# Making the 8-to-16 doubling's sums by two accumulating transfers, with other vector work between it and the next doubling

## The chip, the cores and the metric

The kernel runs on one core of one Trainium2 chip. A core has five engines that run side by side, each through its own list of instructions in order: TensorE (PE, matrix products), VectorE (DVE, elementwise work), ScalarE (ACT, activations), GpSimd (POOL, elementwise work and the issue of some transfers) and SyncE (SP, which issues most transfers). They wait for each other by semaphores. The metric is the device time of one execution in microseconds. Less is better.

## The reference

Two layers, each a state-space convolution and a gated feed-forward network, act on x of shape 1 x 2048 x 512:

```python
def _A_ref(u, A_re, A_im, B_re, B_im, C_re, C_im, log_dt, Dskip):
    dt = jnp.exp(log_dt)[:, None]
    A, Bc, Cc = A_re + 1j * A_im, B_re + 1j * B_im, C_re + 1j * C_im
    P = jnp.exp((dt * A)[:, :, None] * jnp.arange(L)[None, None, :])      # (512, 128, 2048)
    K = jnp.einsum("dn,dnl,dn->dl", Cc, P, dt * Bc).real                  # convolution kernel
    ...                                          # y = causal convolution of u with K, by FFT
    return y + u * Dskip[None, None, :]

def _B_ref(x, w_gate, w_up, w_down):
    return (_silu(x @ w_gate) * (x @ w_up)) @ w_down

for _ in range(2):
    x = x + _A_ref(_layernorm(x), ...)
    x = x + _B_ref(_layernorm(x), ...)
```

What the change touches is the making of K, the 2048 taps of 512 filters out of 128 complex exponentials each. It is done once and used by both layers.

## The kernel before

**Stages.** The first stage, some 320 us, makes K and its spectra. The rest, which this change does not edit, is eight blocks (two layers of four blocks of 512 rows) of convolution by spectra (`ssm`) and feed-forward network (`ffn`).

**How K is made.** The 512 filters are split into eight chunks of 64. A lag l is written as 32a + b. For one chunk the *large factor* is the power with exponent 32a (tiles `re`, `im` of 65 columns and `mu`), and the *small factor* is the power with exponent b times the coefficient (tile `g`, 128 x 2 x 32 x 64: real and imaginary part, 32 powers, 64 filters). `lags` multiplies the two on PE (lines 509 and 510, 128 small products a chunk into `pk`), ACT copies the result to `ks` (line 515), `spread` lays it out (525, 527, result `kp`), ACT copies that to `kt` (1001), and `spectra` turns it into spectra (`pw`, 546), which ACT (555, tile `s`), POOL (557 and 563) and SP (569) store.

**The parts on the vector engine, chunk by chunk.** Each is a Python generator that gives up control at every `yield`:

- `gen_turns` (365, 368) and `gen_reduce` (`rd`; ACT lines 376 and 382, then DVE lines 385 and 388) form the angles of a chunk and take off whole turns, which leaves a remainder. Line 388 is six instructions, for 16, 8, 4, 2, 1 and 1 powers. This is the "remainder work" and belongs to the chunk two ahead.
- `gen_trig` (ACT lines 395, 396, 397) takes sine and cosine of these remainders in three groups: first `xr`, `xi`, which need 385; then the group of 16 powers, which needs the first 388; then the rest, which needs the other five. `gen_exp` and `gen_mags` (ACT 405 and 441) make the magnitudes.
- `gen_e` (`ge`; 450, 450, 453, 453, 456, 459, 459) builds the large factor of the next chunk.
- `gen_g` (`gg`) builds the small factor of the next chunk by doubling. From power 1 it forms powers 2 to 4 (477 to 481), then from 4 powers 8 and from 8 powers 16 (485 to 489, once for n = 4 and once for n = 8), then from 16 powers 32 (492 to 499). One doubling is a complex product: g times the real part of a step factor, plus the other half of g times its imaginary part (tile `btl`). Up to 16 powers, DVE makes the two sums itself (488, 489). In the last doubling, POOL issues two transfers that add a product tile onto `g` in memory (494 and 499).

**What sets the order.** Between lines 899 and 1100 the instructions of ACT, DVE and PE run in the order in which the Python code issues them. Loop 958 goes over the chunks: iteration i multiplies chunk i on PE, builds `g` and the large factor of chunk i + 1 and the remainders of chunk i + 2 on DVE. The tuple in line 986 says how the generators take turns there. Before the loop, chunk 0 has a tuple of its own (line 929). POOL and SP, and all engines after line 1100, are ordered by a scheduler that works from its own model of times.

Of the kernel before, what the change touches and what calls it, by code (L numbers as in the profile page):

```python
# [16 lines left out]
OP = mybir.AluOpType  # L17
# [64 lines left out]
def kernel(ctx, tc, x, a_re, a_im, b_re, b_im, c_re, c_im, log_dt, d_skip,  # L82
                           w_gate, w_up, w_down, c_ef, c_ei, c_ek, c_am, c_eh, c_eih, out):
    nc = tc.nc
    V, A, G, PE = nc.vector, nc.scalar, nc.gpsimd, nc.tensor
# [9 lines left out]
    def tl(shape, name, tag, dt=F32):  # L95
        return sb.tile(shape, dt, name=name, tag=tag, bufs=BUFS[tag])
# [347 lines left out]
    def gen_e(ts):  # L444


        re, im, mu = ts[:3]
        half = [[t.rearrange("p (g h d) a -> p g h d a", g=4, h=2)[:, :, o] for t in ts[:3]] for o in range(2)]
        for r, m, u in half:
            V.tensor_tensor(m[..., :32], m[..., 64:32:-1], r[..., :32], OP.mult)  # L450
            yield
        for r, m, u in half:
            V.tensor_tensor(r[..., :32], r[..., 64:32:-1], r[..., :32], OP.mult)
            yield
        yield
        V.scalar_tensor_tensor(im[:, :, 33:64], im[:, :, 33:64], -1.0, mu[:, :, 1:], OP.mult, OP.mult)
        yield
        for r, m, u in half:
            V.tensor_tensor(r[..., 33:64], r[..., 33:64], u[..., 1:], OP.mult)
            yield  # L460

    def gen_g(ch, ts, g):

        re, im, mu, xz, mz, t16 = ts
        w_ = w0[:, :, ch * DC:(ch + 1) * DC]
        for t in xz:
            V.tensor_tensor(t, t, mz, OP.mult)
        yield
        tm, th_ = tmp
        V.tensor_tensor(g[:, :, 0], w_, re[:, :, 64].unsqueeze(1).to_broadcast([P, 2, DC]), OP.mult)  # L470
        V.tensor_tensor(tm[:, :, 0], w_[:, ::-1], im[:, :, 64].unsqueeze(1).to_broadcast([P, 2, DC]), OP.mult)
        yield
        V.tensor_tensor(g[:, 0, 0], g[:, 0, 0], tm[:, 0, 0], OP.subtract)
        V.tensor_tensor(g[:, 1, 0], g[:, 1, 0], tm[:, 1, 0], OP.add)
        yield
        zr, zi = (t[:, :3].unsqueeze(1).to_broadcast([P, 2, 3, DC]) for t in xz)
        V.tensor_tensor(g[:, :, 1:4], g[:, :, 0:1].to_broadcast([P, 2, 3, DC]), zr, OP.mult)
        V.tensor_tensor(tm[:, :, :3], g[:, ::-1, 0:1].to_broadcast([P, 2, 3, DC]), zi, OP.mult)
        yield
        V.tensor_tensor(g[:, 0, 1:4], g[:, 0, 1:4], tm[:, 0, :3], OP.subtract)  # L480
        V.tensor_tensor(g[:, 1, 1:4], g[:, 1, 1:4], tm[:, 1, :3], OP.add)
        for n in (4, 8):
            yield
            zr, zi = (t[:, ZP.index(n)].unsqueeze(1).unsqueeze(1).to_broadcast([P, 2, n, DC]) for t in xz)
            V.tensor_tensor(g[:, :, n:2 * n], g[:, :, 0:n], zr, OP.mult)
            V.tensor_tensor(tm[:, :, :n], g[:, ::-1, 0:n], zi, OP.mult)
            yield
            V.tensor_tensor(g[:, 0, n:2 * n], g[:, 0, n:2 * n], tm[:, 0, :n], OP.subtract)
            V.tensor_tensor(g[:, 1, n:2 * n], g[:, 1, n:2 * n], tm[:, 1, :n], OP.add)
        yield  # L490
        zr, zi = (t[:, NZ - 1:].to_broadcast([P, 16, DC]) for t in xz)
        V.tensor_tensor(g[:, 1, 16:], g[:, 1, :16], zr, OP.mult)
        V.tensor_tensor(th_, g[:, 0, :16], zi, OP.mult)
        G.dma_start(g[:, 1, 16:], th_, accum_op=OP.add)
        yield
        tl_ = tm.rearrange("p i s d -> p (i s) d")
        V.tensor_tensor(g[:, 0, 16:], g[:, 0, :16], zr, OP.mult)
        V.scalar_tensor_tensor(tl_, g[:, 1, :16], -1.0, zi, OP.mult, OP.mult)
        G.dma_start(g[:, 0, 16:], tl_, accum_op=OP.add)
        yield  # L500
# [12 lines left out]
    def spread_in(pk):  # L513
        ks = tl([P, 4, 16, 16], "ks", "nn")
        A.activation(ks, pk.rearrange("p d (c a) -> p a c d", a=4), AF.Copy)
        return ks
# [78 lines left out]
    def take(it, n):  # L595
        for _ in range(n):
            next(it, None)
# [301 lines left out]
    with tc.manual_schedule(engines={mybir.EngineType.Activation, mybir.EngineType.DVE, mybir.EngineType.PE}):  # L899
# [19 lines left out]
        gg = gen_g(0, ts[0], gs[0])  # L919
        ge, tn, rd = gen_e(ts[0]), gen_turns(1, ts[1]), gen_reduce(ts[1])  # L920
# [37 lines left out]
        for i in range(NCH - 1):  # L958
            if mags:
                take(mags, 1)  # L960
            pk = lags(ts[i], gs[i])
            more = i + 2 < NCH
            tn = rd = f = iter(())
            if more:
                ts[i + 2] = gen_tiles(i + 2)
                tn = gen_turns(i + 2, ts[i + 2])
            gs[i + 1] = tl([P, 2, 32, DC], "g", ("gb", "ga")[i % 2])
            gg, ge = gen_g(i + 1, ts[i + 1], gs[i + 1]), gen_e(ts[i + 1])
            take(ex, 100)
            if mags:  # L970
                take(mags, 2)
            take(sp, 2)
            norm_units(3, 9)
            norm_units(0, 0)
            ks = spread_in(pk)
            if mags:
                take(mags, 1)
            if i % 2 == 0 and 0 < i < NCH - 2:
                parts(i + 2)
                turned()  # L980
            for g in (gg, tn, gg, tn):
                take(g, 1)
            if more:
                rd = gen_reduce(ts[i + 2])
                next(rd)
            for g in (gg, gg, ge, gg, ge, gg, gg, rd, rd, ge, rd, rd, ge, rd, rd, rd, rd):
                take(g, 1)
            while tops:
                tops.pop(0)()
            take(sp, 1)  # L990
            take(gg, 2)
            kp = spread(i, ks)
            if more:
                f = second(*sec[i])
                next(f)
            take(gg, 2)
            if more:
                tr = gen_trig(ts[i + 2])
                take(tr, 1)
            kt = kt2[:, 0]  # L1000
            A.activation(kt, kp, AF.Copy)
            take(tr, 1)
            take(f, 1)
            take(tr, 1)
            if more:
                sp = spectra(i, kt, 0, NB)
                take(sp, 1)
                ex = gen_exp(i + 2, ts[i + 2])
                take(ex, 100)
                mags = gen_mags(i + 2, ts[i + 2])  # L1010
                take(mags, 2)
                norm_units(3, 9)
                take(sp, 2)
                norm_units(0, 0)
                take(mags, 2)
                take(sp, 2)
                sizes(i, kt, ks)
                take(ge, 4)
                take(gg, 1)
                while tops:  # L1020
                    tops.pop(0)()
                ts[i] = gs[i] = None
            else:
                sizes(i, kt, ks)
                take(ge, 4)
                take(gg, 1)
# [119 lines left out]
```

## Time and profile before

| what | value |
|---|---|
| median of three runs | 1188.11 us (1188.05 to 1190.89) |
| the profiled execution, its own time | 1194.56 us |
| its span in the profile | 1192.8 us |
| busy: PE, DVE, ACT, POOL | 1108.3, 1026.5, 618.0, 185.0 us |
| stage that makes K: chunk 0 alone | about 0 to 57 us |
| loop over the chunks, by the start of `lags` on PE | 58.64, 93.04, 124.39, 155.46, 188.23, 219.15, 250.62 us |

The profile is of one execution. A row of its timeline gives a start, a duration, the engine, the line, the operation, output<-input, and in brackets how long the engine was idle before it and who released it. Durations of one engine overlap a little, because an instruction starts before the one ahead has drained, so the step from one start to the next is what an instruction costs in a row. A row of the waits gives who waited for whom, the total in us, the number of times and the longest one. A row of the transfers gives the number, the size of one and the median time from issue to landing.

### The profile page before, as it was taken

What the parts mean: (1) busy time and instruction counts of PE and PEld (TensorE: products, weight loads), DVE (VectorE), ACT (ScalarE), POOL (GpSimd) and SP (SyncE); (2) the same over time, 40 slices, a digit from 0 to 9 for tenths busy, and PEclk for the clock granted to TensorE, in tenths of its full rate; (3) what the DMA queues carried; (4) which work ended last, traced back from release to release, by engine and by line L of the source; (5) the groups of instructions that cost most, each with busy time, mean ns of one, the idle gap of its engine ahead of it and who ended that gap; (6) DMA issues with size and microseconds to landing.
All of it is one profiled execution on the core that took longest, in us unless ns stands there. A gap on an engine that the chain in (4) does not pass through costs nothing.

```text
span 1192.8 us, 25266 instructions
## 1 busy us (share of the span) xinstructions
PE 1108.3 (93%) x10268; PEld 861.2 (72%) x10268; DVE 1026.5 (86%) x1621; ACT 618.0 (52%) x1166; POOL 185.0 (16%) x238
## 2 busy tenths in 40 slices
PE   2889999889887989999999999999999999999998
PEld 2767776667875767768677787868687686867875
DVE  7989999997879999999999999999992899983211
ACT  6998887862355544537743523655432553224211
POOL 3105454343310011202100000211000010000000
PEclk9989999999989999999999999999999999999999
DMA  6444445577497326432344354324434134312000
GB/s 234 141 107 127 114 119 127 126 181 201 141 297 221 109 89 163 161 111 89 85 152 146 115 165 142 111 81 150 140 123 133 45 115 128 125 46 45 15 23 18
DMA packets 139031, 147.95 MB, mean 124 GB/s; under 512 B 77921, under 2 KB 87137, under 8 KB 138914
## 3 DMA queue, kind: packets, MB, share of 16 engines
q1 hardware_dynamic: 134050, 129.56, 35.8%
q0 software_dynamic: 4864, 16.78, 5.9%
q8 instruction: 80, 1.31, 0.5%
q14 instruction: 37, 0.30, 0.1%
HBM read 99.24 MB, written 28.31 MB: 107 GB/s over the span
## 4 chain that ended last, share of the span: by engine, by line
PE 35%; DVE 26%; issue 5%; ACT 3%; DMA 2%; POOL 2%; SPq 1%; DVEq 0%; ACTq 0%; POOLq 0%
PE pgu L860 6%; PE pgu L861 6%; PE pgu L862 6%; DVE t L736 4%; PE py L874 4%; PE py L875 4%; PE py L876 3%; DVE yk L739 3%; DVE yk L736 3%; PE pi L755 3%; PE pf L270 2%; DVE z L226 2%; DVE sg L866 2%; POOL rs L221 2%; DVE bt L226 1%
## 5 line engine op out<-in xcount | busy, mean ns | idle before, releaser
L860 PE MATMUL pgu<-mix,wsl 128*128 128x256 f16 x1280 | 350.2, 274 | 5.3 <-DVE sg L866 3.6
L862 PE MATMUL pgu<-mix,wsl 128*128 128x256 f16 x1280 | 350.3, 274 | 3.6 <-DVE wsl L632 3.6
L861 PE MATMUL pgu<-mix,wsl 128*128 128x256 f16 x1280 | 350.2, 274 | 0.0
L874 PE MATMUL py<-wsl,hh 128*128 128x512 f16 (+1 forms) x352 | 135.5, 385 | 8.9 <-DVE sgr L836 3.1
L861 PEld LDWEIGHTS <-wsl 128*128 128x128 f16 x1280 | 125.7, 98 | 21.8 <-issue 5.8
L862 PEld LDWEIGHTS <-wsl 128*128 128x128 f16 x1280 | 125.7, 98 | 19.1 <-DVE wsl L632 3.9
L860 PEld LDWEIGHTS <-wsl 128*128 128x128 f16 x1280 | 125.7, 98 | 15.8
L876 PE MATMUL py<-wsl,hl 128*128 128x512 f16 (+1 forms) x352 | 135.2, 384 | 1.3 <-DVE hl L868 1.3
L865 ACT ACTIVATE sg<-pgu,sc 128x512 f32<-128x512 f32 x80 | 54.5, 682 | 135.4 <-PE pgu L862 116.5
L736 DVE TENSOR_TENSOR t<-uu,w 128x1024 f32<-128x1024 f32 x96 | 117.0, 1219 | 8.2 <-DMA uu<-udr 7.9
L875 PE MATMUL py<-wsl,hh 128*128 128x512 f16 x320 | 123.3, 385 | 0.0
L739 DVE TENSOR_TENSOR yk<-yk,t 128x1024 f32<-128x1024 f32 x96 | 116.9, 1218 | 0.2
L866 DVE SCALAR_TENSOR_TENSOR sg<-pgu,sc,sg 128x512 f32<-128x512 f32 x80 | 59.7, 746 | 51.0 <-ACT sg L865 50.8
L546 PE MATMUL pw<-kt,ek 128*128 128x256 f32 (+2 forms) x420 | 98.6, 373 | 0.0
L755 PE MATMUL pi<-yl,mix 128*128 128x256 f16 x672 | 91.4, 273 | 1.7 <-ACT yl L744 1.4
L546 PEld LDWEIGHTS pw<-kt,ek 128*128 128x128 f32 x420 | 78.7, 195 | 9.5
L867 ACT ACTIVATE hh<-sg 128x512 f16<-128x512 f32 x80 | 50.0, 625 | 57.5 <-DVE sg L866 57.4
L221 POOL TENSOR_TENSOR rs<-mv,mhalf 128x2 f32<-128x2 f32 (+1 forms) x21 | 38.3, 1824 | 263.2 <-ACT mv L220 255.8
L270 PE MATMUL pf<-z,eh 128*128 128x256 f16 x576 | 74.6, 273 | 1.4 <-ACT z L260 1.4
L755 PEld LDWEIGHTS <-mix 128*128 128x128 f16 x672 | 65.2, 98 | 13.0 <-issue 2.0
L736 DVE TENSOR_TENSOR yk<-u,w0r 128x1024 f32<-128x1024 f32 x56 | 68.2, 1218 | 0.3 <-ACT u L272 0.3
L875 PEld LDWEIGHTS <-hh 128*128 128x128 f16 (+1 forms) x352 | 34.8, 99 | 46.2 <-issue 11.7
(240 smaller groups left out, 2245.8 us busy)
## 6 DMA issues: line engine op xcount, KB each, us to landing
w<-wdr SPq DMA_DIRECT2D x96, 256.0 KB, 2.7
uu<-udr SPq DMA_DIRECT2D x96, 256.0 KB, 3.0
udr<-u POOLq DMA_DIRECT2D x32, 256.0 KB, 2.9
wdr<-wo SPq DMA_DIRECT2D x96, 64.0 KB, 2.5
udr<-u SPq DMA_DIRECT2D x16, 256.0 KB, 2.2
g<-tmp POOLq DMA_DIRECT2D x8, 512.0 KB, 4.5
g<-btl POOLq DMA_DIRECT2D x8, 512.0 KB, 5.9
n<-ndr SPq DMA_DIRECT2D x16, 256.0 KB, 3.0
```

What stands on the lines that cost most here:

```text
L270: PE.matmul(pf[:, o], lhsT=e, rhs=m, start=k == 0, stop=k == len(terms) - 1)
L546: PE.matmul(pw[:, i], lhsT=e, rhs=kt[:, :, c + 4 * k0:4 * k1:4, :].rearrange("p g k d -> p k g d"), start=c == 0, stop=c == 3)
L736: V.tensor_tensor(t, uu.unsqueeze(1).to_broadcast([P, 2, 2, HD]), w.unsqueeze(2).to_broadcast([P, 2, 2, HD]), OP.mult)
L739: V.tensor_tensor(yk, yk, t, OP.add)
L755: PE.matmul(pi[:, o], lhsT=e, rhs=m, start=k == 0, stop=k == len(terms) - 1)
L860: PE.matmul(o, lhsT=wgu(wi, k, 0)[:, fs], rhs=nh[:, k], start=k == 0, stop=False)
L861: PE.matmul(o, lhsT=wgu(wi, k, 0)[:, fs], rhs=nlo[:, k], start=False, stop=False)
L862: PE.matmul(o, lhsT=wgu(wi, k, 1)[:, fs], rhs=nh[:, k], start=False, stop=k == 3)
L866: V.scalar_tensor_tensor(sg, pgu[:, 1], sc6[:, 4:5], sg, OP.mult, OP.mult)
L874: PE.matmul(py[:, r], lhsT=hh[:n, f, rc], rhs=wd(f, 0)[:n], start=f == 0, stop=False)
L875: PE.matmul(py[:, r], lhsT=hh[:n, f, rc], rhs=wd(f, 1)[:n], start=False, stop=False)
L876: PE.matmul(py[:, r], lhsT=hl[:n, f, rc], rhs=wd(f, 0)[:n], start=False, stop=f == FT - 1)
```

## The change

Only the doubling from 8 to 16 powers and its place change. Where DVE made two products of 128 x 1024 and two sums of 128 x 512, it now makes four products of 128 x 512, and POOL issues two transfers of 256 KB that add the product tile `btl` onto the upper half of `g`, as in the last doubling. In the loop, this doubling moves ahead of the remainder work, and one step each of the large factor's work (the second line 450, the second line 453) moves behind parts of the remainder work. Both steps of the last doubling now stand ahead of `spread`; before, the 8-to-16 doubling stood there. The generator has one step less, so the tuple of chunk 0 (line 929), which is not edited, takes its steps otherwise too. The lines of the new kernel are 486 to 491 for the new doubling and 500 to 507 for the last one, which was 492 to 499.

```diff
         for n in (4, 8):
             yield
             zr, zi = (t[:, ZP.index(n)].unsqueeze(1).unsqueeze(1).to_broadcast([P, 2, n, DC]) for t in xz)
+            if n == 8:
+                V.tensor_tensor(g[:, 1, 8:16], g[:, 1, :8], zr[:, 1], OP.mult)
+                V.tensor_tensor(tm[:, 1], g[:, 0, :8], zi[:, 1], OP.mult)
+                G.dma_start(g[:, 1, 8:16], tm[:, 1], accum_op=OP.add)
+                V.tensor_tensor(g[:, 0, 8:16], g[:, 0, :8], zr[:, 0], OP.mult)
+                V.scalar_tensor_tensor(tm[:, 0], g[:, 1, :8], -1.0, zi[:, 0], OP.mult, OP.mult)
+                G.dma_start(g[:, 0, 8:16], tm[:, 0], accum_op=OP.add)
+                continue
...
-            for g in (gg, gg, ge, gg, ge, gg, gg, rd, rd, ge, rd, rd, ge, rd, rd, rd, rd):
+            for g in (gg, gg, ge, gg, gg, gg, gg, rd, rd, ge, rd, rd, ge, rd, rd, rd, rd, ge):
                 take(g, 1)
...
-            take(gg, 2)
```

Chunk 0, ahead of the loop, on DVE before (`g` is the small factor, `btl` and `tmp` are product tiles, `im` the remainders of chunk 1, `t_171` its angles):

```order
L385 TENSOR_TENSOR xi<-xi,xr 128x384
L485 TENSOR_TENSOR g<-g,xr 128x2x512
L486 TENSOR_TENSOR btl<-g,xi 128x1024
L388 SCALAR_TENSOR_TENSOR im<-t_171,re 128x64x16
L488 TENSOR_TENSOR g<-g,btl 128x512
L489 TENSOR_TENSOR g<-g,btl 128x512
L388 SCALAR_TENSOR_TENSOR im<-t_171,re 128x64x8
L492 TENSOR_TENSOR g<-g,xr 128x1024
L493 TENSOR_TENSOR tmp<-g,xi 128x1024
L388 SCALAR_TENSOR_TENSOR im<-t_171,re 128x64x4
L497 TENSOR_TENSOR g<-g,xr 128x1024
L498 SCALAR_TENSOR_TENSOR btl<-g,xi 128x1024
```

The same place with the change:

```order
L385 TENSOR_TENSOR xi<-xi,xr 128x384
L486 TENSOR_TENSOR g<-g,xr 128x512
L487 TENSOR_TENSOR btl<-g,xi 128x512
L489 TENSOR_TENSOR g<-g,xr 128x512
L490 SCALAR_TENSOR_TENSOR btl<-g,xi 128x512
L388 SCALAR_TENSOR_TENSOR im<-t_171,re 128x64x16
L500 TENSOR_TENSOR g<-g,xr 128x1024
L501 TENSOR_TENSOR tmp<-g,xi 128x1024
L388 SCALAR_TENSOR_TENSOR im<-t_171,re 128x64x8
L505 TENSOR_TENSOR g<-g,xr 128x1024
L506 SCALAR_TENSOR_TENSOR btl<-g,xi 128x1024
L388 SCALAR_TENSOR_TENSOR im<-t_171,re 128x64x4
```

Here only one instruction, the first line 388, stands between the new doubling and the last one. The new L500 waits for the first of the two transfers, L501 for the second.

In the loop, iteration 1 (chunk 2's small factor), on DVE before:

```order
L385 TENSOR_TENSOR xi<-xi,xr 128x384
L388 SCALAR_TENSOR_TENSOR im<-t_972,re 128x64x16
L453 TENSOR_TENSOR re<-re 128x4x8x32
L388 SCALAR_TENSOR_TENSOR im<-t_972,re 128x64x8
L388 SCALAR_TENSOR_TENSOR im<-t_972,re 128x64x4
L453 TENSOR_TENSOR re<-re 128x4x8x32
L388 SCALAR_TENSOR_TENSOR im<-t_972,re 128x64x2
L388 SCALAR_TENSOR_TENSOR im<-t_972,re 128x64 x2
L485 TENSOR_TENSOR g<-g,xr 128x2x512
L486 TENSOR_TENSOR btl<-g,xi 128x1024
L488 TENSOR_TENSOR g<-g,btl 128x512
L489 TENSOR_TENSOR g<-g,btl 128x512
```

The same place with the change:

```order
L489 TENSOR_TENSOR g<-g,xr 128x512
L490 SCALAR_TENSOR_TENSOR btl<-g,xi 128x512
L385 TENSOR_TENSOR xi<-xi,xr 128x384
L388 SCALAR_TENSOR_TENSOR im<-t_976,re 128x64x16
L450 TENSOR_TENSOR im<-im,re 128x4x8x32
L388 SCALAR_TENSOR_TENSOR im<-t_976,re 128x64x8
L388 SCALAR_TENSOR_TENSOR im<-t_976,re 128x64x4
L453 TENSOR_TENSOR re<-re 128x4x8x32
L388 SCALAR_TENSOR_TENSOR im<-t_976,re 128x64x2
L388 SCALAR_TENSOR_TENSOR im<-t_976,re 128x64 x2
L453 TENSOR_TENSOR re<-re 128x4x8x32
L500 TENSOR_TENSOR g<-g,xr 128x1024
```

The new doubling has moved ahead of line 385, and ten instructions stand between it and the last doubling.

On POOL with the change, the same iteration (`s_982` and `s_1059` are the third and the fourth spectrum of the chunk before):

```order
L565 COPY w0r<-s_982 128x2x64
L571 TENSOR_TENSOR wo<-s_982 128x192 x2
L488 DMA g<-btl 128x512
L491 DMA g<-btl 128x512
L407 MEMSET re 128x64
L369 MEMSET im 128x64
L565 COPY w0r<-s_1059 128x2x64
L571 TENSOR_TENSOR wo<-s_1059 128x192 x2
L502 DMA g<-tmp 128x1024
L507 DMA g<-btl 128x1024
```

The two new issues stand behind the third spectrum's work and ahead of the fourth's. ACT and PE keep their order in this whole stage, and SP does but for a few neighbouring transfers. In the later blocks the scheduler, whose model sees other times, has exchanged some neighbouring instructions of all engines but POOL.

## The prediction

> **What bounds the kernel now.** I read the busy time by stage first, since the change lies in the stage that makes K. The row gives window, length, then busy time (and instructions) of PE, weight loads, DVE, ACT, POOL, then the PE clock and the transfers' share. The window is about one turn of the loop, from one start of `lags` to the next.
>
> ```profile
> 92.00:124.00 32.00, 29.00 (x395) 22.11 (x394) 31.07 (x38) 26.89 (x43) 16.96 (x21) 1.00 0.52 125
> ```
>
> DVE is busy 31.07 of 32 us, PE 29.00 and ACT 26.89. From this alone, DVE sets the pace. But a busy engine is not yet one that others wait for. So the second view is who waited for whom: ACT from 51 to 249 us (first four rows), PE from 69 to 249 us (two rows), DVE from 57 to 274 us (last four).
>
> ```profile
> ACT ks L515 <- PE pk L510: 15.4, 5, 3.5
> ACT mu L441 <- PE pm L438: 8.4, 5, 3.0
> ACT re L441 <- PE pm L438: 2.2, 6, 0.4
> ACT re L395 <- DVE im L388: 1.1, 1, 1.1
> PE nrm L320 <- ACT sq L316: 9.0, 6, 1.7
> PE pk L510 <- issue: 4.6, 4, 1.2
> DVE xi L385 <- ACT xr L376: 2.6, 2, 2.2
> DVE xr L467 <- ACT mzp L405: 1.9, 1, 1.9
> DVE im L388 <- ACT re L382: 1.3, 3, 0.4
> DVE im L450 <- ACT re L415: 0.9, 1, 0.9
> ```
>
> ACT and PE wait for each other, and DVE waits for ACT. For DVE nobody waits, except ACT once, 1.1 us, at the start of chunk 0's third sine. So the pace is set by a ring of ACT and PE:
>
> ```profile
> 98.88 1.02 ACT L515 ACTIVATE ks<-pk 128x1024 f32<-128x1024 f32 x1 [2.66 <-PE pk L510]
> 118.26 1.51 ACT L316 ACTIVATE sq<-st 128x512 bf16<-128x512 f32 x3
> 118.92 1.21 PE L320 MATMUL nrm<-sq,onesb 128*128 128x512 bf16 x3 [1.67 <-ACT sq L316]
> 124.39 0.37 PE L509 MATMUL pk<-re,g 128*32 128x64 f32 x8
> 130.27 1.02 ACT L515 ACTIVATE ks<-pk 128x1024 f32<-128x1024 f32 x1 [3.13 <-PE pk L510]
> ```
>
> ACT is without a gap from 98.88 to its squares at 118.26. PE has waited for these, then runs without a wait, but for its own issue, to the end of `lags`, for which ACT has waited. That closes at 130.27, after 31.4 us, with no DVE work in it. DVE has nearly the same period, which is why it looks full.
>
> **The change part by part.** The profiled execution took 1194.56 us, 1.8 more than its span of 1192.8 and 6.45 more than the median of 1188.11. I sum against 1194.56 and carry the difference to the median.
>
> *The vector work itself.* One 8-to-16 doubling, with the start of what follows it:
>
> ```profile
> 108.12 1.21 DVE L485 TENSOR_TENSOR g<-g,xr 128x1024 f32<-128x1024 f32 x1
> 109.26 1.21 DVE L486 TENSOR_TENSOR btl<-g,xi 128x1024 f32<-128x1024 f32 x1
> 110.50 0.69 DVE L488 TENSOR_TENSOR g<-g,btl 128x512 f32<-128x512 f32 x1
> 111.11 0.69 DVE L489 TENSOR_TENSOR g<-g,btl 128x512 f32<-128x512 f32 x1
> 111.83 1.23 DVE L492 TENSOR_TENSOR g<-g,xr 128x1024 f32<-128x1024 f32 x1
> ```
>
> From 108.12 to 111.83 it costs 3.71 us. Four instructions of 128x512 take its place. The row at 110.50 is followed after 0.61, the row at 111.11, whose successor needs its result, after 0.72. So 3 x 0.61 + 0.72 = 2.55, and DVE saves 1.16 us a chunk, 9.3 in eight. In the loop none of it is on the ring, so it goes into DVE's wait for ACT at line 385. If DVE were the bound, all of it would count.
>
> *The move.* In the loop, 2.55 us of doubling take the place of one line 450 ahead of line 385 (1.14, the step from 109.26 back to 108.12 for the same size): DVE arrives there 1.4 later, but it began the chunk 3.71 - 1.14 = 2.6 earlier. Behind line 385 one line 450 comes ahead of the small remainders, which ACT's third sine needs:
>
> ```profile
> 107.13 1.07 DVE L388 SCALAR_TENSOR_TENSOR im<-t,re 128x128 f32<-128x128 f32 x3
> 111.81 1.11 ACT L395 ACTIVATE re<-im 128x1024 f32<-128x1024 f32 x1
> ```
>
> They end at 108.2, ACT reaches the sine at 111.81: 3.6 us of room, of which the move takes 1.14. It costs nothing. With that cover gone, each further us would be one on the ring.
>
> *The transfers in the loop.* Sixteen issues of about 0.87 us (below) fall on POOL, for which no row of ACT or PE waits. The new issue stands behind the third spectrum on POOL:
>
> ```profile
> 99.20 1.05 POOL L563 TENSOR_TENSOR wo<-s 128x192 f32<-128x192 f32 x1
> 101.23 0.56 DVE L385 TENSOR_TENSOR xi<-xi,xr 128x384 f32<-128x384 f32 x1 [0.37 <-ACT xr L376]
> ```
>
> So it leaves at 100.25 and the second at about 101.4. The last doubling follows line 385 by 8.0 us: 108.12 - 101.23 = 6.9 before, and 1.14 for line 450. That is 109.3, while even the price of the large transfers, 4.5 and 5.9, would land them at 104.8 and 107.3. It costs nothing. Queued behind a late one would be L500, L501 and all of DVE, which ACT would feel only after the room above. In chunk 7, with no remainder work, only three instructions (3.4 us) stand between, and a stall of 1 us is possible. There the next user is `lags` on PE, which PE reaches late (the last fence of this part).
>
> *The transfers in chunk 0.* Here the one wait of ACT for DVE lies:
>
> ```profile
> 40.23 1.21 DVE L485 TENSOR_TENSOR g<-g,xr 128x1024 f32<-128x1024 f32 x1
> 47.71 0.63 DVE L388 SCALAR_TENSOR_TENSOR im<-t,re 128x256 f32<-128x256 f32 x1
> 48.25 1.22 DVE L497 TENSOR_TENSOR g<-g,xr 128x1024 f32<-128x1024 f32 x1
> 50.52 0.75 DVE L388 SCALAR_TENSOR_TENSOR im<-t,re 128x128 f32<-128x128 f32 x3
> 51.30 1.12 ACT L395 ACTIVATE re<-im 128x1024 f32<-128x1024 f32 x1 [1.06 <-DVE im L388]
> 48.11 1.08 POOL L494 DMA_DIRECT2D g<-tmp  x1 [12.59 <-DVE tmp L493]
> g<-tmp POOLq DMA_DIRECT2D x8, 512.0 KB, 4.5
> g<-btl POOLq DMA_DIRECT2D x8, 512.0 KB, 5.9
> g<-btl POOLq DMA_DIRECT2D x1, 512.0 KB, 7.6
> udr<-u SPq DMA_DIRECT2D x1, 256.0 KB, 2.0
> q0 software_dynamic: 257, 0.99, 17.5%
> ```
>
> The last remainder ends at 51.27 and ACT starts at 51.30 after 1.06 of waiting. From there ACT runs into the ring, so what DVE gains or loses here (at most 1.06 of gain) moves the whole ring. New order from 40.23: products at 40.23, 40.84, 41.45, 42.06, the remainder of 16 powers at 42.70, ready for L500 at 43.84. L487 ends at 40.84 + 0.69 = 41.53, and POOL starts an issue 0.3 later (48.11 against an end at 47.79): 41.83. L491 goes at 42.75 + 0.3 = 43.05.
>
> No row shows an accumulation of 256 KB. From below: the fastest 256 KB at all, 2.0. From above: the 512 KB ones, 4.5 and 5.9, or 7.6 for one beside heavy traffic (the third `g<-btl` row, window 40 to 57). The q0 row (packets, MB, share of 16 engines, window 90 to 121) says that 0.99 MB occupy 17.5% of 31 us, so a transfer of 512 KB occupies 2.7 us and one of 256 KB 1.35 less. I take 4.5 - 1.35 = 3.15 for the first, 3.3 for the second. They land at 45.0 and 46.35. L500 starts at 45.0, L501 at 46.35 (1.2 and 0.2 of stall). Then 1.14 (L501), 0.6 (128x512), 2 x 1.14 (L505, L506), 0.54 (47.71 to 48.25) and 0.75: the remainders end at 51.66, 0.4 later than 51.27. With 2.0: L500 at 43.84, L501 at 45.05, the end at 50.35, 0.9 earlier. With 4.5 and 5.9: L501 at 48.95, the end at 54.25, 3.0 later.
>
> The Trainium skill (DMA: Bandwidth & Descriptors, Anatomy of one DMA — SWDGE (gpsimd) path) gives such a transfer 2.0 us plus its bytes over 436 GB/s, which is an estimate of 2.6 us for 256 KB; the remainders would end at 50.95 by it, 0.3 earlier. It gives 3.2 for 512 KB where the row has 4.5, so I go by the row.
>
> *The end of the stage.* The ring's lead must carry to the rest:
>
> ```profile
> 273.74 1.22 DVE L736 TENSOR_TENSOR yk<-mix,w0r 128x1024 f32<-128x1024 f32 x1
> 276.29 0.37 PE L509 MATMUL pk<-re,g 128*32 128x64 f32 x8
> 289.34 0.69 DVE L716 TENSOR_TENSOR dd<-bb,pi 128x512 f32<-128x512 f32 x1 [3.35 <-PE pi L755]
> ```
>
> DVE leaves the stage at 273.74, PE begins chunk 7's `lags` at 276.29 with no wait, and at 289.34 DVE waits 3.35 us for PE. A DVE that is earlier here waits longer. Gain: nothing.
>
> *Exchanged neighbours in the later blocks.* The largest wait of PE among such instructions is this one, so I bound it by 3.1 both ways and take 0:
>
> ```profile
> PE py L874 <- DVE sgr L836: 3.1, 1, 3.1
> ```
>
> **Sum:** 1194.56 + 0.4 = 1195.0 for such an execution, 1188.11 + 0.4 = 1188.5 for the median.
>
> **The rivals.** *DVE is the bound after all.* For it speaks that DVE is full. Then 8 x 1.16 = 9.3 us come off, less 1.4 of stall in chunk 0: 1180.2. Against it: the waits. It needs a DVE wait of ACT or PE that the profile books elsewhere, such as PE's 1.2 us of "issue" in `lags`, once a chunk; that alone would be worth 8 x 1.16 at most. The Trainium skill (Perfetto Trace Analysis, Identifying the Most-Contended Engine) says that the engine with the highest occupancy is the one to optimize first. By that rule this rival holds; the trace agrees with the occupancy, not with anyone waiting for it.
>
> *Chunk 0's transfers land late.* That ends slower: each us of landing beyond 3.1 of the second one is a us for L501, the remainders, ACT's sine and the ring. At 7.6, as L499's took in the same stretch: 43.05 + 7.6 = 50.65, then 5.3 to the remainders' end at 55.95, 4.7 later: 1192.8. It passes 0.3% (3.6 us) from a landing of 6.5. Against it: L499's was issued at 50.9, beside other traffic.
>
> *POOL holds the new issues in the loop.* If they landed after DVE reaches L500 in every chunk, and by more than the 2.5 us of room left at ACT's sine, the ring would stretch by the rest. By the sum above, a transfer must take 9 us (109.3 - 100.25) to delay DVE at all. One us in each of six chunks would give 1194.
>
> **How the numbers follow.** The forecast has 0.74, DVE as the bound 0.13, late landing in chunk 0 0.09, POOL in the loop 0.04. About 0.3%, 3.6 us, is what a measurement of this kernel can tell from no change. Of the forecast, 0.68 lies within it, 0.02 under and 0.04 over, by the later blocks. With all of the second as faster, and of the last two 0.09 as slower and 0.04 within: faster 0.15, same 0.72, slower 0.13. The forecast's own range is 0.9 + 3.1 down and 3.0 + 3.1 up, 1184.5 to 1194.6, its upper end needing both at once. I give 1184.0 to 1193.0, which leaves out most of the second case and little else.
>
> **What would show it.** Right: `lags` still starts every 31.0 to 31.4 us; DVE's share in the loop's windows falls, and it waits for ACT's line 376 at line 385 in nearly every chunk; L500 and L501 stall in chunk 0 alone, about 1.2 and 0.2 us; ACT's third sine starts at about 51.7. Wrong: a period of about 30.2 us (DVE was the bound); L500 waiting in every chunk (POOL); ACT's third sine at 54 or later (late landing).

## The result

| | median | range | executions |
|---|---|---|---|
| before | 1190.33 us | 1188.05 to 1192.69 | 6 |
| with the change | 1197.32 us | 1194.05 to 1198.25 | 6 |

The change makes the kernel slower: the ratio is 1.0055, with a 95% interval of 1.0036 to 1.0074, which is +6.5 us (4.3 to 8.8). The prediction was 1188.5 us, range 1184.0 to 1193.0. It stands on the first three executions of before (median 1188.11); with the three taken beside the change the median is 1190.33, so 2.2 us of the miss lie in that base. In two later rounds of measurements the same kernel gave +8.9 us (5.8 to 12.0) and +7.3 us (5.4 to 9.0). Two executions at a low granted clock, one of the change (1306 us at 0.85) and one of an experiment (1647 us at 0.66), where the others have 0.98 to 0.99, are left out of all differences. The profiled execution of the change is the fastest of its six (1194.05 us, span 1192.2), and that of before (1194.56 us) is slower than all of its timed ones, so the two spans hide the difference. It must be read from stretches inside the traces and from timed kernels.

### The profile page after: what moved, and what is told of

It reads as the page before. It is cut to its first block, busy times and chain, and to the rows that moved or that the text cites. A ratio compares the mean times of both kernels' runs of the same rounds, so it can differ in the third digit from the quotient of the medians.

```text
span 1192.2 us, 25294 instructions
## 1 busy us (share of the span) xinstructions
PE 1106.9 (93%) x10268; PEld 860.9 (72%) x10268; DVE 1017.9 (85%) x1621; ACT 618.6 (52%) x1166; POOL 190.8 (16%) x254
## 4 chain that ended last, share of the span: by engine, by line
PE 35%; DVE 23%; issue 6%; DMA 4%; ACT 3%; POOL 2%; SPq 1%; DVEq 0%; ACTq 0%; POOLq 0%
PE pgu L868 6%; PE pgu L869 6%; PE pgu L870 6%; PE py L882 4%; PE py L883 4%; PE py L884 3%; DVE t L744 3%; DVE yk L747 3%; PE pi L763 3%; PE pf L270 2%; DVE z L226 2%; DVE yk L744 2%; DMA mix<-nn 2%; POOL rs L221 1%; DVE sg L874 1%
## 5 line engine op out<-in xcount | busy, mean ns | idle before, releaser
L752 ACT ACTIVATE yl<-mix,sy 128x512 f16<-128x512 f32 x56 | 40.1, 716 | 52.9 <-DVE mix L749 52.7
```

## The profile after

The first view is who waited for whom in the stage that makes K (engine, line, what it waited for: total, times, longest). First ACT from 51 to 249 us (three rows), then PE from 69 (one), then DVE from 57 to 274 us (three).

```profile
ACT ks L523 <- PE pk L518: 16.2, 5, 3.4
ACT mu L441 <- PE pm L438: 6.7, 5, 1.3
ACT re L395 <- DVE im L388: 2.1, 1, 2.1
PE nrm L320 <- ACT sq L316: 8.7, 6, 1.7
DVE tmp L501 <- DMA g<-btl: 4.6, 1, 4.6
DVE xi L385 <- ACT xr L376: 3.2, 4, 1.6
DVE im L388 <- ACT re L382: 1.7, 4, 0.4
```

ACT and PE wait for each other as before. The page counts 1017.9 us of busy DVE, 8.6 less than before, and DVE waits for ACT more often at line 385 (four times, where it was two). Two rows are new in size: ACT's third sine waits 2.1 us for DVE (1.1 before), and DVE waits 4.6 us for an accumulating transfer.

The second view is the timeline: the first row is chunk 1's `lags`, the second chunk 6's.

```profile
94.58 0.37 PE L517 MATMUL pk<-re,g 128*32 128x64 f32 x8
253.05 0.37 PE L517 MATMUL pk<-re,g 128*32 128x64 f32 x8
```

The same two in the kernel before:

```profile
93.04 0.37 PE L509 MATMUL pk<-re,g 128*32 128x64 f32 x8
250.62 0.37 PE L509 MATMUL pk<-re,g 128*32 128x64 f32 x8
```

Five turns take 158.5 us, 31.7 each; before 157.6, 31.5 each. The loop has not become faster, although DVE has 1.2 us less to do in each turn.

Chunk 0, from the same timeline of the change:

```profile
41.29 1.08 POOL L488 DMA_DIRECT2D g<-btl  x1 [6.31 <-DVE btl L487]
42.49 0.88 POOL L491 DMA_DIRECT2D g<-btl  x1
44.80 1.23 DVE L500 TENSOR_TENSOR g<-g,xr 128x1024 f32<-128x1024 f32 x1 [1.49 <-DMA g<-btl]
46.45 1.23 DVE L501 TENSOR_TENSOR tmp<-g,xi 128x1024 f32<-128x1024 f32 x1 [0.42 <-DMA g<-btl]
51.78 1.12 ACT L395 ACTIVATE re<-im 128x1024 f32<-128x1024 f32 x1 [2.08 <-DVE im L388]
```

The transfers free their readers 3.5 us (44.80 - 41.29) and 4.0 us (46.45 - 42.49) after the start of their issue. DVE stalls 1.5 and 0.4 us, and ACT's third sine waits 2.08 us where it waited 1.06: chunk 0 comes 1.0 us later into the ring.

Chunk 7, from the timeline (POOL, DVE, SP):

```profile
258.00 0.89 POOL L488 DMA_DIRECT2D g<-btl  x1 [1.45 <-DVE btl L487]
259.20 0.87 POOL L491 DMA_DIRECT2D g<-btl  x1 [0.32 <-DVE btl L490]
268.50 1.23 DVE L501 TENSOR_TENSOR tmp<-g,xi 128x1024 f32<-128x1024 f32 x1 [4.62 <-DMA g<-btl]
259.00 0.41 SPq L1041 DMA_DIRECT2D mix<-in_c_ei_dram  x1
259.46 1.02 SPq L677 DMA_DIRECT2D mix<-udr  x1
```

The second transfer is issued at 259.20 and frees L501 at 268.50, after 9.3 us. Just then SP starts two large loads for the first block, of 768 and 1024 KB. The stall is hidden in this execution: chunk 7's `lags`, the next user, starts 25.7 us after chunk 6's (253.05), as it did before (276.29 after 250.62).

```profile
278.73 0.37 PE L517 MATMUL pk<-re,g 128*32 128x64 f32 x8
```

The later blocks differ at one place. In the order of their rows the two kernels are the same on ACT, DVE, SP and POOL from 300 us on, but for one stretch, from 458 to 516 us: 7 rows of SP, 9 of ACT and 13 of DVE have moved there, and the rows of PE differ only there too. There SP reads two tiles of x back (`n<-xdr`, `xg<-xdr`, 1024 KB each) and transposes the last strip of the feed-forward network (`hh<-sgr`, `hl<-sgr`). The timeline with the change, SP and then ACT:

```profile
464.68 0.38 SPq L232 DMA_DIRECT2D n<-xdr  x1
465.11 0.50 SPq L232 DMA_DIRECT2D xg<-xdr  x1
465.78 2.77 SPq L849 DMA_TRANSPOSE hh<-sgr  x2
...
470.12 2.46 SPq L849 DMA_TRANSPOSE hl<-sgr  x2
...
476.66 0.69 ACT L873 ACTIVATE sg<-pgu,sc 128x512 f32<-128x512 f32 x1 [5.53 <-DMA hl<-sgr]
```

SP's timeline before:

```profile
465.28 2.40 SPq L841 DMA_TRANSPOSE hh<-sgr  x2
467.79 2.44 SPq L841 DMA_TRANSPOSE hl<-sgr  x2
...
472.68 0.43 SPq L232 DMA_DIRECT2D n<-xdr  x1
473.15 0.51 SPq L232 DMA_DIRECT2D xg<-xdr  x1
```

The transfers issued from 462 to 476 us, with their number and median time to landing, after:

```profile
hh<-sgr SPq DMA_TRANSPOSE x2, 7.8
hl<-sgr SPq DMA_TRANSPOSE x2, 5.0
```

And before:

```profile
hh<-sgr SPq DMA_TRANSPOSE x2, 2.8
hl<-sgr SPq DMA_TRANSPOSE x2, 2.3
```

Before, the transposes go first. With the change the loads go first, the transposes land in 7.8 and 5.0 us instead of 2.8 and 2.3, and ACT waits 5.5 us for them: its tile `sg` is taken from the same buffers as `sgr` (lines 839 and 872), so it can only be written when the transposes have read `sgr`. DVE, which is full there, then waits for ACT, as the waits of the change from 462 to 484 us say:

```profile
DVE sg L874 <- ACT sg L873: 2.3, 1, 2.3
```

`xg<-py` is the DVE instruction that adds the network's result onto x. The stretch from its third to its fifth time (line 879 before, 887 after; the expectations below call it a yk evacuation, which it is not) holds the moved rows but the last few, and shows the price. Window, length, busy time of PE, weight loads, DVE, ACT, POOL; first after:

```profile
444.72:509.71 64.99, 59.68 (x520) 46.76 (x521) 60.62 (x98) 32.75 (x65) 8.75 (x8) 0.97 0.53 158
```

Then before:

```profile
446.90:509.14 62.24, 59.70 (x520) 46.23 (x521) 60.53 (x98) 32.86 (x65) 9.12 (x8) 0.97 0.56 163
```

The same work takes 2.75 us more. What follows it, from the fifth `xg<-py` to the last, takes 678.7 us (to 1188.38) where it took 679.8 (to 1188.92), so the loss is not made up later.

## The experiments

All times are differences from the kernel before on the same chip, with their 95% intervals. Two later orders matter. *Old* is the order of the blocks after line 1100 in the kernel before, *new* that of the changed kernel. Which one a kernel gets is decided by the scheduler and not by the edit itself. There are just these two: from 300 us on, the rows of ACT, DVE, SP and POOL come in the same order in all kernels called new, and in the same in all called old, and the two differ from about 458 to 525 us alone.

### First: the change taken apart

Theory A held chunk 0's lateness and the later order responsible, theory B the loop's transfers.

**Loop only** (old order):

```diff
-            if n == 8:
+            if n == 8 and ch:
```

> Chunk 0 keeps the old doubling (sums by VectorE, no transfer); chunks 1 to 7 have the new one. The blocks after the first stage keep the order of the kernel before. Theory A (the changed kernel is slow by chunk 0's late transfers, about 2 us, and by the exchanged neighbours in the later blocks, about 4 us): no change, within 2 us of before. Rival B (the extra transfers and the new order in the loop cost the time): 4 to 6.6 us slower than before.

Measured +2.7 us (0.2 to 5.2).

**Chunk 0 only** (new order): the loop's tuple and steps as before, and

```diff
-            if n == 8:
+            if n == 8 and not ch:
```

> Only chunk 0 has the new doubling; the loop is that of the kernel before. The later blocks have the exchanged neighbours of the changed kernel. Theory A (chunk 0 about 2 us, later blocks about 4 us): 6 to 7 us slower, like the changed kernel. Rival B (the loop): 0 to 2 us slower.

Measured +3.9 us (1.9 to 6.0).

**The new places with the sums by DVE** (old order), no added transfer:

```diff
-                V.tensor_tensor(g[:, 1, 8:16], g[:, 1, :8], zr[:, 1], OP.mult)
...
+                V.tensor_tensor(g[:, :, 8:16], g[:, :, 0:8], zr, OP.mult)
+                V.tensor_tensor(tm, g[:, ::-1, 0:8], zi, OP.mult)
+                V.tensor_tensor(g[:, 0, 8:16], g[:, 0, 8:16], tm[:, 0], OP.subtract)
+                V.tensor_tensor(g[:, 1, 8:16], g[:, 1, 8:16], tm[:, 1], OP.add)
```

> The changed kernel's places and tuples, but the two sums of the doubling made by VectorE as before, with no added transfer. The later blocks keep the order of before. Theory A: no change, within 2 us. If the new places in the loop (one large-factor step ahead of the remainders) cost the time: 4 us or more slower. If VectorE bounds the loop: no change, since its work is that of before.

Measured +0.2 us (-2.0 to 2.4): the move alone costs nothing.

**The change with the old order**, got by making a small product of chunk 0 three times (0.84 us more on DVE, which the scheduler's model answers with the old order):

```diff
-        V.tensor_tensor(tm[:, :, 0], w_[:, ::-1], im[:, :, 64]...
+        for _ in range(3 if ch == 0 else 1):
+            V.tensor_tensor(tm[:, :, 0], w_[:, ::-1], im[:, :, 64]...
```

> The changed kernel with one small product (128x128) of chunk 0 made three times, which gives the later blocks the order that they have in the kernel before; the two repeats themselves cost 0.6 us of VectorE in chunk 0. Theory A: 2 us (chunk 0) + 0.6, so 2.7 us slower than before. If chunk 0 or the loop alone makes the loss, the later order counts for nothing: 7 us slower.

Measured +3.6 us (1.5 to 5.6), of which up to 0.8 are the extra products. ACT's third sine waits 2.1 us, as in the change, so chunk 0 is as late.

Neither theory came out whole. The loop cost 2.7 us where A allowed 2, and chunk 0 with the new order 3.9 where B allowed 2 and A expected 6 to 7; the intervals are too wide to throw either out. The loop-only trace pointed to chunk 7, where DVE stalled 3.9 and 1.5 us. That became theory C (chunk 7's transfers, late beside the first block's loads) against D (a little in each chunk).

### Second: chunk 7, and chunk 0 without the new order

**Chunks 1 to 6 only**, and **chunk 7 only** (both old order). Chunks with the old doubling keep the old tuple:

```diff
-            if n == 8:
+            if n == 8 and 0 < ch < 7:
```

```diff
-            if n == 8:
+            if n == 8 and ch == 7:
```

> The new doubling in chunks 1 to 6 alone; chunk 0 and chunk 7 keep the old one, and the later blocks have the order of the kernel before. Theory C (the loss of the loop-only kernel, 2.7 us, lies in chunk 7, whose two new transfers run beside the first loads of the next block, landed 9 us after their issue and held DVE 5 us): nothing is left of the loss, 0 +- 1.5 us against before, and no wait of DVE for L488's or L491's transfer. Theory D (each chunk's two extra transfers or their issues on POOL cost the ring a little, 2.7/7 = 0.4 us a chunk): +2.3 us, spread over the starts of lags.

> The new doubling in chunk 7 alone, again with the later order of the kernel before. Theory C: +2.5 us (+1.5 to +3); DVE stalls 4 to 5.5 us in all at L500 and L501, both transfers take 7 to 10 us to land, and the first mix<-pt of block 0 comes 2.4 to 3 us later after the start of chunk 6's lags than the 76.3 us of the kernel before. Theory D: +0.4 us, and mix<-pt where it was.

Measured +1.9 us (-1.0 to 4.8) for chunks 1 to 6 and +9.3 us (6.8 to 11.7) for chunk 7 alone. In the latter, the waits of DVE and PE read:

```profile
DVE g L500 <- DMA g<-btl: 5.4, 1, 5.4
DVE tmp L501 <- DMA g<-btl: 0.8, 1, 0.8
PE pk L517 <- POOL wo L571: 2.8, 1, 2.8
```

Its transfers issued from 255 to 272 us (number, size, median time to landing):

```profile
mix<-udr SPq DMA_DIRECT2D x1, 1024.0 KB
mix<-in_c_ei_dram SPq DMA_DIRECT2D x1, 768.0 KB, 5.4
g<-btl POOLq DMA_DIRECT2D x2, 256.0 KB, 10.2
```

DVE stalls 6.2 us (5.4 and 0.8). PE's wait stands against POOL, whose last instruction before it is the issue of the last transfer of `g`; it is that transfer which `lags` needs. So C had chunk 7's late transfers right, but this price is three times the loop-only kernel's, which contains the same transfers, and the trace shows a third of it: chunk 7's `lags` starts 28.6 us after chunk 6's, 2.9 more than before. DVE reaches them about 1 us later after the start of chunk 6's `lags` than in the loop-only kernel, since chunk 6 has not saved its 1.2 us.

**Chunk 0 only, real half first** (old order): the two halves of the new doubling change places, so the last doubling waits for the second transfer instead of the first. The lines with a plus stood behind the other three.

```diff
+                V.tensor_tensor(g[:, 0, 8:16], g[:, 0, :8], zr[:, 0], OP.mult)
+                V.scalar_tensor_tensor(tm[:, 0], g[:, 1, :8], -1.0, zi[:, 0], OP.mult, OP.mult)
+                G.dma_start(g[:, 0, 8:16], tm[:, 0], accum_op=OP.add)
                 V.tensor_tensor(g[:, 1, 8:16], g[:, 1, :8], zr[:, 1], OP.mult)
                 V.tensor_tensor(tm[:, 1], g[:, 0, :8], zi[:, 1], OP.mult)
                 G.dma_start(g[:, 1, 8:16], tm[:, 1], accum_op=OP.add)
```

> The new doubling in chunk 0 alone, with its two halves exchanged: the real half is made and sent first, the imaginary half second. The last doubling reads the imaginary half first, so it waits for the second transfer; and the later blocks happen to come out in the order of the kernel before. It separates chunk 0's lateness from the later order, which came together in the chunk-0-only kernel (+3.9 us). If chunk 0's lateness passes to the end whole: DVE stalls 3.1 us ahead of the last doubling (1.9 in the changed kernel), ACT waits 3.3 us at its third sine (1.06 before), +2.2 us in all, and the stretch between the third and the fifth yk evacuation of block 1 stays at 62.3 us. If the late order alone made the chunk-0-only kernel slow: 0 +- 1.

Measured +3.9 us (1.5 to 6.3). The waits are as expected, 3.1 on DVE and 3.2 on ACT, which would be +2.1, inside the interval. The stretch of the later blocks stayed at 61.8 us.

**The change again:**

> The changed kernel once more, on the chip of the three others: a second profile and more times of it. Sum of the parts as they stand now: chunk 0 +1.0, chunk 7 about +2.5, the later order +1.8 to +2.7: +5.3 to +6.2 us. In its profile, if these are the parts: DVE stalls 1.5 and 0.4 us in chunk 0 and 4 to 5.5 us in chunk 7, ACT's third sine waits 2.1 us, and the stretch between the third and the fifth yk evacuation is 64 to 65 us.

Measured +8.9 us (5.8 to 12.0), with stalls of 1.7 and 0.2 us in chunk 0, of 4.2 and 1.4 in chunk 7, and 66.7 us in the later stretch.

### Third: is it the traffic, and is it chunk 7?

**All chunks but 7** (new order), `if n == 8 and ch < 7`:

> The changed kernel with the old doubling in chunk 7 alone; its later blocks keep the order of the changed kernel. Theory C (the largest part of the loss sits in chunk 7): chunk 0 +1.0, the later order +1.8 to +2.7, nothing from chunks 1 to 6: +2.8 to +3.7 us against before, as the chunk-0-only kernel (+3.9), and well under the +9.0 of the changed kernel on the chip before. Without C, that is if chunk 7 costs nothing here: +7 to +9.

Measured +7.4 us (4.5 to 10.4). That contradicts C: without chunk 7's transfers the loss is still there.

**Without the two loads**, the sums by DVE in one kernel and chunk 7's transfers in the other (both old order):

```diff
-        nc.sync.dma_start(ei, c_ei)
+        for k, m in ((0, 3), (4, 4)):
+            A.activation(mix[:, k * D:(k + m) * D].rearrange("p (m d) -> p m d", m=m),
+                         rho.unsqueeze(1).to_broadcast([P, m, D]), AF.Copy, scale=0.0)
...
-                    nc.sync.dma_start(u4, udr[0][0, 0].rearrange("q p i d -> p q i d"))
```

> The partner of the next run: the new places with sums by DVE (no added transfer), and without the two large loads into mix that start block 0 (the 768 KB of c_ei and the first 1024 KB of udr are left out; two copies of 128x1536 and 128x2048 by ACT fill the tile instead, so block 0's results are not the reference's). Expected -2 to +3 us against before: two loads less, 3 to 4 us more on ACT, which is busy only 5.4 of 18 us there. DVE waits for no transfer in chunk 7.

> The chunk-7-only kernel (+9.3 us) without the same two loads (768 KB of c_ei, 1024 KB of udr, filled by ACT instead); later blocks in the order of the kernel before. If the traffic of these loads makes the new transfers late: they land in 4 to 6 us (10.2 in the chunk-7-only kernel), DVE stalls 0 to 1.5 us (6.2), and the time is within 2 us of the partner's. If the transfers are late for another reason (the queue's own pace, POOL): they take 8 to 10 us again, DVE stalls 4 to 6 us, and it is 5 to 9 us over the partner.

Measured +5.4 us (3.6 to 7.1) and +11.8 us (7.7 to 15.8). The transfers of the second kernel, from 255 to 272 us:

```profile
g<-btl POOLq DMA_DIRECT2D x2, 256.0 KB, 3.4
```

With the loads gone the same transfers land in 3.4 instead of 10.2 us, and DVE does not stall. So the traffic of SP's loads made them late (four loads of `st`, 172 KB each, which SP issues there in the chunk-7-only kernel, do not come in this window either). The times say nothing: in both kernels ACT came to wait for a weight load `st`, 5.1 us in the first and 13.1 in the second, a disturbance that the experiment brought in itself.

**A late DVE without any transfer** (old order): in chunk 7, the second product of the old doubling is made four times.

```diff
-            V.tensor_tensor(tm[:, :, :n], g[:, ::-1, 0:n], zi, OP.mult)
+            for _ in range(4 if n == 8 and ch == 7 else 1):
+                V.tensor_tensor(tm[:, :, :n], g[:, ::-1, 0:n], zi, OP.mult)
```

> The kernel before, no new transfer anywhere; in chunk 7 alone the second product of the 8-to-16 doubling (128x1024, 1.14 us) is made four times, so that DVE comes to the last doubling 3.4 us later. Later blocks in the order of the kernel before. If DVE's lateness is what passes from chunk 7 to the end: L459's end is 3.4 us later after the start of chunk 6's lags, chunk 7's lags wait for the last transfer (1.5 to 2.5 us), and the time is +2 to +6 us. If DVE's lateness is hidden and only the contention among transfers costs: 0 to +1 us. My prediction took DVE to have about 3 us of room here (3.35 us of waiting at line 716), which would also give 0 to +0.5.

Measured +2.4 us (0.1 to 4.8). In the trace PE waits 1.8 us ahead of chunk 7's `lags`, which starts 27.6 us after chunk 6's instead of 25.7. So 3.4 us of lateness pass in part; the room of about 3 us that the prediction saw here is not there in full.

### Fourth: a square

Transfers or DVE's sums in chunk 0 and in chunk 7, with chunks 1 to 6 and all places as in the change. The edit, with `ch == 7`, `ch == 0`, or both as the condition, at each of the two transfers:

```diff
-                G.dma_start(g[:, 1, 8:16], tm[:, 1], accum_op=OP.add)
+                if ch == 7:
+                    V.tensor_tensor(g[:, 1, 8:16], g[:, 1, 8:16], tm[:, 1], OP.add)
+                else:
+                    G.dma_start(g[:, 1, 8:16], tm[:, 1], accum_op=OP.add)
```

> The changed kernel, all in its places, but chunk 7's two sums made by DVE instead of by transfers; later order of the changed kernel. If chunk 7's transfers carry about 3 us of the loss: +3.8 us against before (chunk 0 +1.0, later order +2.8), 3 less than the changed kernel of this same call; no stall at L500 or L501 in chunk 7. If the kernel with the old doubling in chunk 7 (+7.4) told the truth and chunk 7 costs nothing: +7.

> The changed kernel with chunk 0's two sums made by DVE; with this the later blocks get the order of the kernel before. Chunk 7 alone is left: +3 us against before (+2 to +4.5), ACT's third sine waits 1.1 to 1.3 us, DVE stalls 5 to 6 us in chunk 7, and the stretch between the third and the fifth yk evacuation is 61.8 to 62.7 us. If chunk 7 costs nothing: 0 +- 1.5.

> The changed kernel with the sums by DVE in chunks 0 and 7, transfers in chunks 1 to 6 alone, later order of the kernel before: every part that is held to cost is out, so 0 +- 1.5 us against before, as the ring theory says of the loop, although DVE is relieved of 6 times 1.2 us. If the transfers of the loop cost by themselves: +2 or more. If DVE's relief paid: -3 or less.

> The changed kernel once more, beside the three, so that each part is read as a difference on one chip. Sum of the parts: chunk 0 +1.0, chunk 7 +3, later order +2.8: +6.8 us (its earlier values are +6.6 and +9.0). The stretch between the third and the fifth yk evacuation 64 to 66.7 us.

| | chunk 7 by transfers | chunk 7 by DVE |
|---|---|---|
| chunk 0 by transfers (new order) | +7.3 (5.4 to 9.0), the change | +7.7 (6.1 to 9.4) |
| chunk 0 by DVE (old order) | +4.4 (2.4 to 6.4) | +2.3 (-0.6 to 5.1) |

In the changed kernel, chunk 7's transfers cost nothing that can be told (7.3 against 7.7). With the old order it is 2 us (4.4 against 2.3), with zero well inside its interval of some 3.5 to each side. Chunk 0 and the new order together cost 5.4 us in one column and 2.9 in the other, each clear of zero.

### Fifth: chunk 0 or the later order

Chunk 0 alone is changed in both kernels. They differ in one line, and by it in the later order.

```diff
-                V.tensor_tensor(g[:, 1, 8:16], g[:, 1, 8:16], tm[:, 1], OP.add)
+                G.dma_start(g[:, 1, 8:16], tm[:, 1], accum_op=OP.add)
```

> Chunk 0 alone is changed: four half products as in the changed kernel, the first sum by a transfer, the second by DVE. The later blocks come out in the order of the changed kernel. DVE waits about 0.9 us for the one transfer at L500, and saves one sum of 0.6 us, so ACT's third sine comes 0.3 us later than in the partner below. If the later order costs by itself: +2.7 us (the stretch between the third and the fifth yk evacuation, 63.6 to 66.7 us against 61.7 to 63.2) and +0.5, so +3 or more against before and +3 against the partner. If it costs nothing and chunk 0's lateness is all: +0.3 to +0.5.

> The partner: the same four half products in chunk 0, both sums by DVE, no new transfer; the later blocks come out in the order of the kernel before. It differs from the run above by one transfer against one sum in chunk 0, and by the later order. 0 to +0.5 us against before under either reading; the stretch between the third and the fifth yk evacuation 61.7 to 63.2 us.

Measured +8.0 us (4.9 to 11.2) with the one transfer and the new order, and -1.0 us (-3.7 to 1.8) without. ACT's third sine waits 1.5 us in the one and 1.4 in the other, so chunk 0 is the same within 0.3 us up to there. What is left by the edit is the later order, the part of theory A that the first round had not isolated. The times differ by 9 us, and the traces give the order a third of it. In the kernel with the new order, the wait for the transposes:

```profile
ACT sg L873 <- DMA hl<-sgr: 4.5, 1, 4.5
```

And the stretch from the third to the fifth `xg<-py`, as a window:

```profile
448.61:513.02 64.41, 58.54 (x520) 45.81 (x521) 60.58 (x97) 32.51 (x65) 8.76 (x8) 1.00 0.54 160
```

In its partner that wait does not occur, and the stretch reads:

```profile
442.12:503.70 61.58, 60.35 (x519) 46.92 (x520) 60.52 (x97) 32.59 (x64) 6.03 (x8) 0.94 0.57 166
```

That is 2.8 us. The two profiled spans differ by 9.0 (1194.8 and 1185.8), and 6.5 of these are there at the first `xg<-py`, ahead of every moved row. The kernel with the one transfer, a load that DVE waits for and the first `xg<-py`:

```profile
343.08 1.23 DVE L744 TENSOR_TENSOR t<-uu,w 128x1024 f32<-128x1024 f32 x1 [7.34 <-DMA uu<-udr]
391.09 0.75 DVE L887 SCALAR_TENSOR_TENSOR xg<-py,sc,xg 128x512 f32<-128x512 f32 x1
```

Its partner:

```profile
336.58 1.23 DVE L744 TENSOR_TENSOR t<-uu,w 128x1024 f32<-128x1024 f32 x1 [2.78 <-DMA uu<-udr]
384.60 0.75 DVE L887 SCALAR_TENSOR_TENSOR xg<-py,sc,xg 128x512 f32<-128x512 f32 x1
```

4.6 of the 6.5 us are this one wait (7.34 against 2.78). Behind the stretch nothing is left: from the fifth `xg<-py` to the last it is 677.9 and 678.2 us.

Over all profiles: in the seven with the new order ACT waits 3.0 to 6.5 us for `hl<-sgr`, and the stretch takes 63.6 to 66.7 us, 64.9 in the mean. In the thirteen with the old order ACT never waits for it, and the stretch takes 61.6 to 63.2 us, 62.2 in the mean. That is 2.7 us at this one place. What follows, to the last `xg<-py`, takes 678.6 and 678.7 us in the mean.

## Why the prediction was wrong

**The step that failed is "Exchanged neighbours in the later blocks".** It took 0, with a bound of 3.1 from the largest wait of PE among such instructions. The new order costs 2.7 us in the traces (64.9 against 62.2 us, seven profiles against thirteen, with no overlap), the largest part of the loss that the runs show. That this lies inside the bound is luck. The bound was made from the wrong engine: it looked at waits of PE for DVE, while what moved was two loads of 1 MB on SP's queue, ahead of four transposes on which a buffer of ACT hung. The trace of before had the rows for it (the two loads with 1024 KB each, and the transposes landing in 2.3 to 2.8 us when nothing stood ahead of them).

**Nearly half of the loss stays open.** Measured and forecast lie 8.8 us apart (1197.3 and 1188.5). Of these, 2.2 are the base, 0.6 chunk 0 (next paragraph) and 2.7 the later order; for the last 3.3 no run shows the step. The timed pairs of new and old order differ by 9 us (about 5 to 13) in the pair of the fifth round, by 3 to 5.5 in three pairs where chunk 0 is later by about 1 us as well (7.3 against 4.4, 7.7 against 2.3, 7.4 against 1.9), and by nothing between chunk 0 alone and its exchanged halves (3.9 and 3.9, the latter with chunk 0 later by 1.1), each with some 3 to 4 us of uncertainty. As far as these traces show, more than the 2.7 us can't be put down to the order of the rows, since it is the same ahead of 458 us, and behind the stretch nothing is lost. The load that made half of the fifth pair's difference kept DVE waiting from 2.8 to 7.9 us around 341 us in kernels of either order, and with one trace for each kernel that cannot be told from chance.

**Chunk 0's transfers** were sized right in the mechanism and a little low in the term: 3.15 and 3.3 us from issue to landing were estimated, 3.5 and 4.0 measured; stalls of 1.2 and 0.2 were forecast, 1.5 and 0.4 came; the ring starts 1.0 us later instead of 0.4. The Trainium skill's figure (DMA: Bandwidth & Descriptors, Anatomy of one DMA — SWDGE (gpsimd) path), an estimate of 2.6 us for 256 KB, lies below all three: the traces have 3.4 with little else under way, 3.5 to 4.0 in chunk 0, and 8.6 to 10.2 in chunk 7 of the kernels with the old order. Going by the row and not by the figure was right: by the figure the remainders would end earlier than before, and they end later. The forecast's own range (1184.5 to 1194.6) counts 0.9 down and 3.0 up from 1188.5, though both were worked out against before; from 1188.11 it is 1184.1 to 1194.2.

**"A stall of 1 us is possible" in chunk 7** was too small by a factor of five, since the step asked how many instructions stand between issue and reader, and not what SP issues at that time. In the changed kernel it costs nothing that can be told, as the step said for its next user: in the three profiles of the change chunk 7's `lags` starts 25.7, 26.8 and 26.1 us after chunk 6's, 25.7 before. With the old order the timed kernels give 2 us (zero inside the interval) and, for chunk 7 alone, 9; the later order begins 190 us behind chunk 7 and can't be the reason. Why chunk 7 alone costs so much more than the loop with chunk 7 in it is only argued (DVE arrives 1 us later, and `lags` then waits 2.8 us), not shown.

**The ring** stands. With the new places and DVE's sums it is +0.2 us, with transfers in chunks 1 to 6 +1.9 (old places in the other chunks) and +2.3 (new places in all), and with nothing but chunk 0's half products -1.0, each with zero in its interval, though the two in the middle relieve DVE of 7 us (6 times 1.16) and their intervals end at 1.0 and 0.6 us of gain. The period of `lags` is 31.7 us where 31.0 to 31.4 was forecast and 30.2 would have shown DVE as the bound. So the rival "DVE is the bound after all" is out, and with it, for this stage, the rule that the engine with the highest occupancy comes first (the Trainium skill, Perfetto Trace Analysis, Identifying the Most-Contended Engine). The rival "POOL holds the new issues in the loop" is out too: in the profile of the change L500 and L501 stall in chunks 0 and 7 alone. "Late landing" in chunk 0 came out at 4.0 us for the second transfer, not 7.6.

The sum that the runs support for the change is 1.0 from chunk 0 and 2.7 from the later order, 3.7 of 6.5 us (4.3 to 8.8). About 3 us are open. A rival for them is the loop: the +1.9 and +2.3 of the kernels with transfers in chunks 1 to 6 would fill most of it, but each has zero in its interval, and the starts of `lags` do not show it: five turns take 159.3 and 157.3 us, 157.6 before, and 159.9 in the chunk-0-only kernel, whose loop is not edited. No kernel of this study is faster than the one before by more than its interval.

## What to carry to other kernels

Where a scheduler orders part of a program, an edit elsewhere can reorder it, and that part is then a change of its own: read the moved instructions on every queue, and price a moved transfer by its size and by what stands behind it, not by the waits that the old order happened to show. To learn what an edit itself is worth, compare kernels that have the same order in the rest, if need be by a harmless extra instruction. And ask where in time the reordered part begins: it can't be charged with what is lost ahead of it. Before moving work off a full engine, find who waits for it; in the loop here nobody did.

## What the runs showed of the hardware that was not expected

- A transfer that adds 256 KB onto a tile landed in 3.4 us (median of two) with little other traffic and in 6.3 to 10.2 us (medians of two, over all kernels that issue them in chunk 7) beside loads of 768 and 1024 KB issued within 2 us of it. In the whole changed kernel it took 4.7 us in the median of sixteen, as long as the 512 KB ones (4.8 and 5.3, both from the page):

```profile
g<-btl POOLq DMA_DIRECT2D x16, 256.0 KB, 4.7
g<-tmp POOLq DMA_DIRECT2D x8, 512.0 KB, 4.8
g<-btl POOLq DMA_DIRECT2D x8, 512.0 KB, 5.3
```

- The first two transposes, issued less than 1 us behind two loads of 1024 KB, landed in 7.8 to 9.1 us (medians of two, seven profiles), against 2.3 to 2.8 us ahead of the loads (thirteen profiles).
- One execution differs from the next by more than most of the parts here: the same changed kernel ran from 1193.45 to 1206.65 us, and in three profiles DVE waited 3.5, 5.5 and 4.7 us for the same load around 341 us.
